# One level of Strassen's algorithm for the last two tiles of a first layer

## The chip, the cores and the metric

The kernel runs on one core of a Trainium2 chip. The metric is the device time of one execution in microseconds (us), as the median of several executions. TensorE (PE) multiplies matrices; VectorE (DVE), ScalarE (ACT) and GpSimd (POOL) work element by element; SyncE (SP) and ACT issue the DMAs. Each engine takes its own instructions strictly in the order in which the program lists them and waits for others by semaphores.

## The reference

Three blocks follow one another. An attention with a feature map gives `x`, 4608 rows of 512 numbers. The second block is the one that this change touches; the third has four more matrix products.

```python
def _moe_ref(x, w_in, w_out):          # x 4608 x 512, w_in 512 x 2048, w_out 2048 x 512
    h = x @ w_in
    g = h - np.tanh(h)
    return (g @ w_out).astype(np.float32)

def _moe2_ref(x, w1, w2, w3, w_out):   # w1, w2 512 x 1024, w3 1024 x 1024, w_out 1024 x 512
    a = x @ w1
    b = x @ w2
    h = a * b @ w3
    return (h @ w_out).astype(np.float32)
```

The weights come in double precision, and float32 accuracy is kept with TensorE's fast float32 format: each operand is split into a high part (the rounded number) and a low part (what the rounding lost), and each product is three matmuls, high by high, low by high, high by low.

## The kernel before

The program has three parts in a row: the attention, the "first layer" (`moe1`, the second block above) and the "second layer" (`moe2`, the third block, which already computes its products with one level of Strassen's algorithm, seven products of half-size blocks for eight; its lines are L840 and L849).

In the first layer all data stand transposed: features on the 128 partitions, tokens along the free axis. The 4608 tokens are nine tiles of 512 (`NB`), and the 2048 hidden features are sixteen blocks of 128 (`NFC`). A step `n` is one block of one tile, so the layer has 144 steps; step `n` is block `n % 16` of tile `n // 16`. In step `n` PE computes `h`, the product of block `n`'s input weights and the tile's x (`mm1`, L501: four slices of the 512 inputs by three matmuls, 12 matmuls of 512 columns), and then the output product of the block two steps earlier (`mm2`, L580: four output parts `y0` to `y3` by three, 12 matmuls of 512 columns that add up in four PSUM banks over the sixteen blocks). In most steps `mm2` takes the eight matmuls that need the high part `gh` first and the four that need the low part `gl` last; in the first and the last block of a tile it goes by output part, and `gl` is needed by the third matmul.

Between the two stands `act_g`: ACT squares `h`, takes its tanh, and makes two more operands for small arguments (L522 to L525); DVE forms `h - tanh(h)`, a polynomial and the choice between them (L529 to L533). `g_parts` then splits the result of the step before: ACT copies out `gh` (L550), and POOL subtracts it to give `gl` (L551). At the end of a tile (in the second step of the next) `y_out` copies the four finished banks to SBUF, three by ACT (L563) and one by DVE (L565), and they are stored to DRAM; the four copies share three buffers named `yo`.

Beside that, a table `extra` hands every step a share of other work: the conversion of weights from double precision (`conv`; POOL's part is L132), their split into two parts (`split`; POOL's part is L617), and for the second layer's first weights the sums that Strassen's algorithm wants (`combos`, eight groups, one every seven steps from step 14 on; POOL's lines L636 to L645). `pieces` converts the other two weights in 48 pieces over 54 steps. The next tile's x is loaded, multiplied by the attention's denominators and split in four slices (`load_x`, `mul_x` L1056, `split_x` L1063). In POOL's program the order within a step is: `gl` of the step before, then the step's share of `extra`, then the x work. What a step's POOL work delays is therefore the next `gl`.

The pool `ps_h` has three PSUM banks for `h`. SBUF arenas (`w`, `late`, `xa`, `xb`, `xn`) hold the weights' two parts, two tiles' x, and the x being prepared. In the last tile the second layer's weights (`w3t`, `wo2`) are loaded into slots as their blocks fall free, and `w34` (L738) begins the second layer while the last two `mm2` wait.

## Time and profile before

| | us |
|---|---|
| median of 3 executions (lowest to highest) | 1654.81 (1654.49 to 1658.12) |
| the profiled execution, its own time | 1654.07 |
| the profiled span, first to last instruction | 1652.3 |
| PE busy in it | 1641.5 |
| DVE, ACT, POOL busy | 1101.6, 935.2, 949.6 |

The time of an execution is the span and some 1.8 us around it. Busy is the time in which at least one instruction of the engine runs. PE's busy time is close to the span, but a matmul's recorded duration is longer than the distance between two of them, since they overlap; the distance is what counts. The first layer runs from 299 us to about 1084 us. TensorE's granted clock is at full speed (1.00) in all of it.

### The profile page before, as it was taken

To read this page: it belongs to the slowest core of one execution; us is meant where nothing else is said; L and a number is where in the kernel's file an instruction comes from. 1 tells how busy PE (TensorE), PEld (TensorE's weight loads), DVE (VectorE), ACT (ScalarE), POOL (GpSimd) and SP (SyncE) were. 2 spreads that over 40 slices of the span, in tenths; PEclk is the share of its full clock that TensorE was granted. 3 is DMA by queue.
4 is the path that set the end of the run, shared out by engine and by line. 5 is a ranking of instruction groups with operands and counts; after the bars stand their busy time and mean duration, and the time that the engine had idled before them with its cause. 6 is when DMAs were issued, how large, how long until landed. Compare 5 with 4: busy or idle time off the path is not lost.

```text
span 1652.3 us, 31982 instructions
## 1 busy us (share of the span) xinstructions
PE 1641.5 (99%) x11702; PEld 1356.1 (82%) x11702; DVE 1101.6 (67%) x1649; ACT 935.2 (57%) x1884; POOL 949.6 (57%) x948
## 2 busy tenths in 40 slices
PE   9999999999999999999999999999999999999999
PEld 7777776788888888888888888888888888889999
DVE  7888887697555555666666665536765756847574
ACT  6788877787767666767777765443232232312221
POOL 6888998596757565656565662254633624515241
PEclk9999999999999999999999999999999999999999
DMA  6566664332333333424353436429768777688886
GB/s 186 179 178 192 190 189 143 101 117 92 110 113 125 112 117 107 128 78 143 106 147 99 141 96 226 140 103 328 220 209 265 207 237 236 184 278 283 285 258 220
DMA packets 159788, 283.64 MB, mean 172 GB/s; under 512 B 20304, under 2 KB 48336, under 8 KB 159632
## 3 DMA queue, kind: packets, MB, share of 16 engines
q1 hardware_dynamic: 146800, 246.31, 47.7%
q10 hardware_dynamic: 12832, 35.30, 6.8%
q8 instruction: 92, 1.51, 0.4%
q14 instruction: 64, 0.52, 0.1%
HBM read 218.32 MB, written 63.21 MB: 170 GB/s over the span
## 4 chain that ended last, share of the span: by engine, by line
PE 91%; DVE 3%; ACT 3%; POOL 1%; DMA 1%; issue 1%; SPq 0%; ACTq 0%; DVEq 0%; POOLq 0%
PE y L580 22%; PE h L501 22%; PE q L840 15%; PE q L849 7%; PE pa L840 6%; PE kv L299 3%; PE o L849 3%; PE p L226 3%; PE o L356 3%; PE h L738 3%; PE o L365 1%; PE tr L266 1%; POOL ks L323 1%; ACT kp L248 1%; DVE dk L237 1%
## 5 line engine op out<-in xcount | busy, mean ns | idle before, releaser
L551 POOL TENSOR_TENSOR gl<-t,gh 128x512 fp32r<-128x512 f32 x144 | 187.0, 1298 | 242.0 <-ACT gh L550 155.2
L529 DVE TENSOR_TENSOR t<-h,t 128x512 f32<-128x512 f32 x144 | 99.3, 690 | 181.8 <-ACT t L523 174.6
L840 PE MATMUL q<-w,w 128*128 128x512 f32 (+1 forms) x960 | 210.8, 367 | 0.2 <-DVE c L912 0.2
L522 ACT ACTIVATE u<-h 128x512 f32<-128x512 f32 x144 | 85.7, 595 | 200.9 <-PE h L501 200.7
L840 PEld LDWEIGHTS q<-w,w 128*128 128x128 f32 x960 | 174.9, 188 | 23.7 <-DVE c L912 1.3
L580 PE MATMUL y<-gh,w 128*128 128x512 f32 x720 | 182.2, 390 | 0.6 <-ACT gh L550 0.6
L580 PEld LDWEIGHTS y<-gh,w 128*128 128x128 f32 x720 | 134.9, 188 | 29.8 <-ACT gh L550 1.0
L530 DVE SCALAR_TENSOR_TENSOR u<-h,u 128x512 f32<-128x512 f32 x144 | 99.4, 691 | 70.1 <-ACT m L525 70.1
L501 PE MATMUL h<-xa,w 128*128 128x512 f32 x600 | 143.9, 389 | 0.0
L902 ACT ACTIVATE c<-pa 128x512 f32<-128x512 f32 (+1 forms) x40 | 22.2, 556 | 194.8 <-PE pa L840 194.8
L501 PEld LDWEIGHTS h<-xa,w 128*128 128x128 f32 x600 | 112.5, 188 | 23.6 <-issue 0.2
L235 DVE TENSOR_REDUCE m<-p 128x4 f32<-128x512 f32 (+1 forms) x145 | 98.7, 681 | 36.9 <-PE p L226 31.9
L501 PE MATMUL h<-xb,w 128*128 128x512 f32 x480 | 115.4, 389 | 0.0
L533 DVE COPY_PREDICATED t<-m,s 128x512 f32<-128x512 uint32 x144 | 109.1, 757 | 4.9
L132 POOL TENSOR_TENSOR et<-et,eraw 128x256 uint32<-128x256 uint32 x104 | 77.9, 749 | 59.0 <-issue 38.6
L580 PE MATMUL y<-gh,late 128*128 128x512 f32 x432 | 111.1, 389 | 0.0
L501 PEld LDWEIGHTS h<-xb,w 128*128 128x128 f32 x480 | 90.1, 188 | 18.8
L525 ACT ACTIVATE m<-u,cs 128x512 f32<-128x512 f32 x144 | 104.0, 722 | 0.0
L524 ACT ACTIVATE s<-u,cs 128x512 f32<-128x512 f32 x144 | 100.2, 696 | 6.2 <-DVE t L533 6.2
L532 DVE SCALAR_TENSOR_TENSOR s<-s,u 128x512 f32<-128x512 f32 x144 | 100.7, 699 | 4.6
L580 PE MATMUL y<-gl,w 128*128 128x512 f32 x360 | 100.5, 390 | 1.1 <-POOL gl L551 1.1
L323 POOL TENSOR_TENSOR ks<-ks,kp 128x256 f32<-128x256 f32 x128 | 95.7, 774 | 9.2 <-ACT kp L248 9.1
(173 smaller groups left out, 3843.9 us busy)
## 6 DMA issues: line engine op xcount, KB each, us to landing
w<-w_d SPq DMA_DIRECT2D x420, 256.0 KB
w_d<-w SPq DMA_DIRECT2D x72, 256.0 KB
qk<-in_qk ACTq DMA_DIRECT2D x30, 576.0 KB
v<-in_v ACTq DMA_DIRECT2D x30, 320.0 KB
num_d<-st SPq DMA_DIRECT2D x128, 72.0 KB
xn<-num_d SPq DMA_DIRECT2D x36, 256.0 KB
eraw<-in_w SPq DMA_DIRECT2D x32, 256.0 KB
eraw<-in_w3t SPq DMA_DIRECT2D x32, 256.0 KB
```

The source lines that it names most:

```text
L323: POOL.tensor_tensor(s, kp[m // G][:, :, m % G, :] if t < 4 else s, x, ALU.add)
L501: PE.matmul(ps, a[:, kk, :], b[kk], start=m == 0, stop=m == 3 * NK - 1)
L524: ACT.activation(s, u, ACTF.Square, bias=c1_sb)
L525: ACT.activation(m, u, ACTF.Relu, bias=lim_sb, scale=-1.0)
L529: DVE.tensor_tensor(t, h, t, ALU.subtract)
L530: DVE.scalar_tensor_tensor(u, h, C2, u, ALU.mult, ALU.mult)
L532: DVE.scalar_tensor_tensor(s, s, C0, u, ALU.add, ALU.mult)
L533: DVE.copy_predicated(t, m.bitcast(U32), s)
L551: POOL.tensor_tensor(gl, t, gh.bitcast(F32), ALU.subtract)
L580: PE.matmul(yy[j][d], w[:, d * 128:(d + 1) * 128], x, start=i == 0 and m == 0, stop=i == NFC - 1 and m == 2,)
L840: PE.matmul(ps, w[:, a, c], x[b][:, kk, :], start=start and m == 0, stop=m == 5, skip_group_check=True)
L849: PE.matmul(ps, w[:, a, c], x[:, b, :], start=start and kk == 0 and n == 0, stop=kk == 3 and n == 2, skip_group_check=True,)
```

## The change

The first seven tiles are computed as before. Tiles 8 and 9 (`JA = 7` and 8 in the program's count) go by `pair`: two blocks at a time, 256 hidden features by 512 inputs by 512 tokens, with one level of Strassen's algorithm. Each of the seven products is 128 features by 256 inputs by 256 tokens, six matmuls of 256 columns (L885), so a pair has 42 matmuls of 256 columns where two steps had 24 of 512. The output products (`y_ops`, L816) stay 24 matmuls of 512 columns; they are kept in a list and issued in portions of 3, 8 and 13 between the products.

The seven sums of weight blocks are prepared during the first tiles by `combos_in`, eight groups, one every seven steps from step 18 on: two DVE additions, four POOL sums and four splits (ACT and POOL) for each, and ten stores to a DRAM buffer `win_d`. In the last two tiles `more_in` loads them back, 512 KB at a time, through a ring of five slots in the weights' own space. The x sums of these tiles are made by `next_x` (`mul` into `xb`, `sums_x`, `split_xk`). The products are added up by one ACT copy and five DVE additions per pair, into the banks X and Y of the three in `ps_h`; Z holds one product alone. The elementwise work of block Y is done within the pair; that of block X is finished in the next pair.

Other edits: `y3` is copied into the x buffer `xn` instead of `yo`, and the x load of a tile begins two steps later (steps 2, 5, 8, 11 of a tile, used two steps later); the 48 pieces are converted over 38 steps instead of 54, a step sooner each, and DVE instead of ACT makes their high parts; the last tile loads seven of the sixteen `w3t` slots during its pairs and nine after them, and one quarter of the second layer's first input last of all.

On PE, the tiles before and after; `h` is the x product's bank, `y_...` the four output banks. Before, one step:

```order
L501 MATMUL h<-xb,late 128x512 x12
L580 MATMUL y_12075<-gh,w 128x512 x2
L580 MATMUL y_12076<-gh,w 128x512 x2
L580 MATMUL y_12077<-gh,w 128x512 x2
L580 MATMUL y_12078<-gh,w 128x512 x2
L580 MATMUL y_12075<-gl,w 128x512
L580 MATMUL y_12076<-gl,w 128x512
L580 MATMUL y_12077<-gl,w 128x512
L580 MATMUL y_12078<-gl,w 128x512
```

And in the changed kernel about half a pair, from its first product on:

```order
L885 MATMUL hX<-late 128x256 x6
L885 MATMUL hZ<-late 128x256 x6
L816 MATMUL y_13456<-gl,w 128x512
L816 MATMUL y_13457<-gl,w 128x512
L816 MATMUL y_13458<-gl,w 128x512
L885 MATMUL hX<-late 128x256 x6
L885 MATMUL hY<-late,w 128x256 x6
L816 MATMUL y_13455<-gh,w 128x512 x2
L816 MATMUL y_13456<-gh,w 128x512 x2
L816 MATMUL y_13457<-gh,w 128x512 x2
L816 MATMUL y_13458<-gh,w 128x512 x2
L885 MATMUL hX<-xa,w 128x256 x6
```

The x products stand in groups of six narrow matmuls, with output products of the pair before between them.

On POOL, step 27, which holds a conversion (`et`), splits (`w`) and a slice of x (`xa`), up to the next `gl`. Before:

```order
L132 TENSOR_TENSOR et<-et,eraw 128x256
L617 TENSOR_TENSOR w<-et,w 128x256 x2
L642 TENSOR_TENSOR et<-et 128x256
L1063 TENSOR_TENSOR xa<-xn,xa 128x512
L551 TENSOR_TENSOR gl<-t,gh 128x512
```

And in the changed kernel, where `eraw` holds the input weights' sums:

```order
L137 TENSOR_TENSOR et<-et,eraw 128x256
L627 TENSOR_TENSOR w<-et,w 128x256 x2
L653 TENSOR_TENSOR et<-et 128x256
L691 TENSOR_TENSOR eraw<-eraw 128x256
L692 TENSOR_TENSOR eraw<-eraw 128x256
L627 TENSOR_TENSOR w<-eraw,w 128x256
L1334 TENSOR_TENSOR xa<-xn,xa 128x512
L556 TENSOR_TENSOR gl<-t,gh 128x512
```

Two sums and one split have come in ahead of the same `gl`.

On DVE, one step of tile 8 before (its last two rows are a piece's conversion):

```order
L529 TENSOR_TENSOR t<-h,t 128x512
L530 SCALAR_TENSOR_TENSOR u<-h,u 128x512
L532 SCALAR_TENSOR_TENSOR s<-s,u 128x512
L533 COPY_PREDICATED t<-m,s 128x512
L124 SCALAR_TENSOR_TENSOR et<-eraw,et 128x256
L121 TENSOR_SCALAR et<-et 128x256
```

And one pair in the changed kernel, from the second of its five sums on; `xb` and `xz` are its temporaries:

```order
L915 TENSOR_TENSOR xb<-hY,xb 128x256
L916 TENSOR_TENSOR hY<-hX,xb 128x256
L843 SCALAR_TENSOR_TENSOR s<-s,xz 128x512
L844 COPY_PREDICATED t<-m,s 128x512
L933 TENSOR_TENSOR hY<-hY,xb 128x256
L935 TENSOR_TENSOR hX<-hX,xb 128x256
L830 TENSOR_TENSOR t<-hY,t 128x512
L831 SCALAR_TENSOR_TENSOR xz<-hY,u 128x512
L843 SCALAR_TENSOR_TENSOR s<-s,xz 128x512
L844 COPY_PREDICATED t<-m,s 128x512
L830 TENSOR_TENSOR t<-hX,t 128x512
L831 SCALAR_TENSOR_TENSOR xz<-hX,u 128x512
```

The sums read PSUM banks, and the two rows on `hX` that release the bank for the next pair stand last, behind all of block Y's work.

The diff, cut:

```diff
+                elif d == 3:
+                    t = words_of("xn", 0, [512])
                 else:
...
-            def conv(src, into):
+            def conv(src, into, spare=True):
...
-                return [c[0], [], c[1] + c[2], c[3] + c[4] + [keep]]
-
-            def split(of, store):
+                return [c[0]] + [[]] * spare + [c[1] + c[2], c[3] + c[4] + [keep]]
+
+            def split(of, store, act=True):
                 o2 = {}

...
+                    if act:
+                        ACT.activation(w[:, 0], t, ACTF.Copy)
+                    else:
+                        DVE.tensor_copy(w[:, 0], t)
...
+            def combos_in(g, at):
+                both = [slots["in", 2 * g + i] for i in range(2)]
+                t = []
+
+                def whole():
+                    for hi, lo in both:
+                        raw = p2.tile([128, cw], I64, tag="eraw", name="eraw", bufs=4).bitcast(F32)
+                        DVE.tensor_tensor(raw, fc_view(hi).bitcast(F32), fc_view(lo).bitcast(F32), ALU.add)
+                        t.extend((raw[:, :cw], raw[:, cw:]))
+                    for q, i, half in ((0, 0, 0), (1, 0, 1), (3, 1, 1)):
+                        for e in range(2):
+                            SP.dma_start(win_d[7 * g + WHICH.index(q)][:, e], fc_view(both[i][e][:, 2 * half:2 * half + 2]).bitcast(F32))
+
+                def sums_1():
+                    POOL.tensor_tensor(t[3], t[2], t[3], ALU.add)
+                    POOL.tensor_tensor(t[2], t[0], t[2], ALU.subtract)
+
+                def sums_2():
+                    POOL.tensor_tensor(t[0], t[3], t[0], ALU.subtract)
+                    POOL.tensor_tensor(t[1], t[1], t[0], ALU.subtract)
+
+                def out(q, i, k):
+                    place(split(lambda: t[i], lambda w: SP.dma_start(win_d[7 * g + WHICH.index(q)], w)), at + k)
+
+                place([[whole], [sums_1], [sums_2]], at)
+                out(6, 2, 2)
+                out(4, 3, 3)
+                out(5, 0, 4)
+                out(2, 1, 4)
+
...
-                place(conv(src, t), at)
-                place(split(lambda: t[0], store), at + 5)
+                place(conv(src, t, False), at)
+                place(split(lambda: t[0], store, False), at + 4)
...
-                piece(*c, 70 + i * 54 // len(todo))
+                piece(*c, 70 + i * 38 // len(todo))
...
+            def more_in():
+                if blocks:
+                    t = words_of(*ring_at[ring_n[0] % len(ring_at)], [2, 2 * cw])
+                    ring_n[0] += 1
+                    n = blocks.pop(0)
+                    src = win_d[n:n + 2].rearrange("q p a n -> p q (a n)")
+                    SP.dma_start(t.bitcast(F32), src)
+                    ring.extend(t[:, q].rearrange("p (a n) -> p a n", a=2) for q in range(2))
+
+            def split_xk(j, k):
+                if (j - JA) % 2 == 0:
+                    t = words_of("w", k * 1024, [2, 512])
+                elif k < 4:
+                    t = words_of("late", 2048 + k * 1024, [2, 512])
+                else:
+                    t = words_of("xa", (k - 4) * 1024, [2, 512])
+                xk[j, k] = t
+                hi, lo = [t[:, e].rearrange("p (a n) -> p a n", a=2) for e in range(2)]
+                ACT.activation(hi, xk["s"][k], ACTF.Copy)
+                POOL.tensor_tensor(lo, xk["s"][k], hi.bitcast(F32), ALU.subtract)
+
+            xa = []
+
+            def next_x(j, i, acts=None):
+                if j + 1 == NB:
+                    return
+                if j + 1 < JA:
+                    if i % 3 == 2 and i > 2:
+                        split_x(j + 1, i // 3 - 1, xa[0])
+                    if i % 3 == 2 and i < 12:
+                        xa[:] = load_x(j + 1, i // 3)
+                    if i % 3 == 1 and i > 1 and i < 14:
+                        mul_x(*xa)
+                    return
+                for k in {7: (0,), 11: (4,)}.get(i, ()):
+                    split_xk(j + 1, k)
+                if i in (4, 6, 8, 10):
+                    POOL.tensor_tensor(raw_x(i // 2 - 2), xa[0], xa[1], ALU.mult)
+                if i in (2, 4, 6, 8):
+                    xa[:] = load_x(j + 1, i // 2 - 1)
+                if i in (9, 11, 12, 13):
+                    sums_x((9, 11, 12, 13).index(i))
+                for k in {12: (6,), 13: (2,), 14: (1, 3), 15: (5,)}.get(i, ()):
+                    split_xk(j + 1, k)
+
...
+                todo = [(d, m) for d in range(NK) for m in range(3)]
+                if first:
+                    todo.sort(key=lambda a: (a[0] // 2, a[1] == 2))
+                elif not last:
+                    todo.sort(key=lambda a: a[1] == 2)
+
...
+            def pair(n, ys):
                 j, i = divmod(n, NFC)
-                if n < n_all:
-                    mm1(n)
-                else:
-                    w34(n - n_all)
...
+                x1, x2 = extra.get(n, []), extra.get(n + 1, [])
+                X, Y, Z = [None] * 3
+                for k in ("XYZ", "YZX", "ZXY")[n // 2 % 3]:
+                    t = ps_h.tile([128, 512], F32, tag="h", name="h" + k)
+                    X, Y, Z = [t if k == q else o for q, o in zip("XYZ", (X, Y, Z))]
+                u2, u3 = [words_of("xb", 3584 + 256 * k, [cw]) for k in range(2)]
+                vb, va = [words_of("xz", 512 * k, [512]) for k in range(2)]
+
+                def product(ps, k, start=False):
+                    w, x = ring.pop(0), xk[j, k]
+                    m = 0
+                    for kk in range(2):
+                        for a, b in ((0, 0), (1, 0), (0, 1)):
+                            PE.matmul(
+                                ps, w[:, a, kk * 128:(kk + 1) * 128], x[:, b, kk * cw:(kk + 1) * cw],
+                                start=start and m == 0, stop=m == 5, skip_group_check=True,
+                            )
+                            m += 1
+                    used[0] += 1
+                    if used[0] % 2 == 0:
+                        more_in()
+
+                product(X[:, :cw], 0, True)
+                ACT.activation(u2, X[:, :cw], ACTF.Copy)
+                product(Z[:, :cw], 1, True)
+                y_some(3)
+                if n == n_a:
+                    g_parts(n_a - 1)
+                    stream.extend(y_ops(n_a - 1, False, True))
+                if left:
+                    g_parts(left["n"] + 1)
+                done = full.pop() if full else None
+                if done:
+                    for d in range(2):
+                        y_move(done, d, True)()
+                    store2 = y_move(done, 2, False)
+                DVE.tensor_tensor(u2, Z[:, :cw], u2, ALU.add)
+                product(X[:, cw:], 2)
+                product(Y[:, cw:], 3, True)
+                if left:
+                    left["sm"] = act_2(left["u"])
+                if done:
+                    store2()
+                DVE.tensor_tensor(u3, Y[:, cw:], u2, ALU.add)
+                DVE.tensor_tensor(Y[:, cw:], X[:, cw:], u3, ALU.add)
+                if done:
+                    y_move(done, 3, False)()
+                end_a()
+                spread(x1, True)
+                spread(x1, False)
+                next_x(j, i)
+                spread(x2, True)
+                spread(x2, False)
+                next_x(j, i + 1)
+                if left:
+                    g_parts(left["n"])
+                for a in ys:
+                    stream.extend(y_ops(*a))
+                y_some(8)
+                product(X[:, :cw], 4)
+                product(Y[:, :cw], 5)
+                DVE.tensor_tensor(Y[:, :cw], Y[:, :cw], u3, ALU.add)
+                product(X[:, cw:], 6)
+                DVE.tensor_tensor(X[:, cw:], X[:, cw:], u2, ALU.add)
+                ub, tb = act_1(Y)
+                sb, mb = act_2(ub)
+                dve_1(Y, tb, ub, vb)
+                dve_2(tb, vb, sb, mb)
+                ua, ta = act_1(X)
+                dve_1(X, ta, ua, va)
+                y_some(13)
+                if n == n_a or ys[-1][2]:
+                    full.append((j - 1, yy.pop(j - 1)))
+                tt[n + 1] = tb
+                left.update(n=n, u=ua, t=ta, v=va)
+
...
+            for n in range(n_a):
+                j, i = divmod(n, NFC)
+                if n == n_a - NFC:
+                    renew("xb")
+                    sums_x(4)
+                if n >= 18 and (n - 18) % 7 == 0 and (n - 18) // 7 < 8:
+                    combos_in((n - 18) // 7, n)
+                mm1(n)
+                act_g(n, mm2(n - LAG) if n >= LAG else None)
+                spread(extra.get(n, []), False)
+                for k in range({n_a - 6: 3, n_a - 4: 2}.get(n, 0)):
+                    more_in()
+                next_x(j, i)
+            renew("xz")
+            stream += y_ops(n_a - 2, False, False)
+            ys = []
+            for n in range(n_a, n_all, 2):
+                j, i = divmod(n, NFC)
+                pair(n, ys)
+                ys = [(n + 1, i == 0, False), (n, False, i == NFC - 2)]
+                if j + 1 == NB:
+                    if i == 2:
+                        load_b(0, ((0, 0), (0, 1), (1, 0)))
+                    if i >= 2:
+                        load_w3t(i // 2 - 1)
...
+            for i in range(7, NFC):
+                load_w3t(i)
+            load_b(0, ((1, 1),))
+            y_some(3)
+            g_parts(left["n"] + 1)
+            left["sm"] = act_2(left["u"])
+            end_a()
+            g_parts(left["n"])
+            w34(0)
+            for f in y_ops(*ys[0]):
+                f()
+            w34(1)
+            for f in y_ops(*ys[1]):
+                f()
+            for d in range(4):
+                y_out((NB - 1, yy[NB - 1]), d)
```

## Rows read from the trace of the kernel before

**Rows 1.** Page, parts 1 and 4: busy time by engine; longest chain by line.
```profile
span 1652.3 us, 31982 instructions
...
PE 1641.5 (99%) x11702; PEld 1356.1 (82%) x11702; DVE 1101.6 (67%) x1649; ACT 935.2 (57%) x1884; POOL 949.6 (57%) x948
...
PE y L580 22%; PE h L501 22%; PE q L840 15%; PE q L849 7%; PE pa L840 6%; PE kv L299 3%; PE o L849 3%; PE p L226 3%; PE o L356 3%; PE h L738 3%; PE o L365 1%; PE tr L266 1%; POOL ks L323 1%; ACT kp L248 1%; DVE dk L237 1%
```

**Rows 2.** Waits of PE, first layer: us in total, times, longest us.
```profile
PE y L580 <- POOL gl L551: 1.1, 2, 0.9
PE y L580 <- ACT gh L550: 0.6, 1, 0.6
```

**Rows 3.** Timeline, PE, a run of the x products: start us, us, instruction, xcount.
```profile
1004.93 2.88 PE L501 MATMUL h<-xa,w 128*128 128x512 f32 x12
```

**Rows 4.** Timeline, PE, 384 columns wide, second layer.
```profile
1500.42 2.24 PE L840 MATMUL q<-w,w 128*128 128x384 f32 x12
```

**Rows 5.** Groups by form: xcount | busy us, mean ns of one | idle us before.
```profile
L840 PEld LDWEIGHTS q<-w,w 128*128 128x128 f32 x960 | 174.9, 188 | 23.7 <-DVE c L912 1.3
L501 PE MATMUL h<-xa,w 128*128 128x512 f32 x600 | 143.9, 389 | 0.0
...
L840 PE MATMUL q<-w,w 128*128 128x384 f32 x384 | 72.0, 334 | 0.2 <-DVE c L912 0.2
...
L356 PEld LDWEIGHTS o<-qp,kvx 128*32 128x32 f32 x1024 | 32.9, 110 | 26.0 <-ACT st L376 1.1
...
L911 DVE TENSOR_TENSOR u<-q,u 128x512 f32<-128x512 f32 x24 | 16.6, 690 | 21.4 <-PE q L840 21.4
...
L911 DVE TENSOR_TENSOR u<-q,u 128x384 f32<-128x384 f32 x16 | 8.9, 557 | 9.5 <-PE q L840 9.5
```

**Rows 6.** Timeline, all engines, an undisturbed step of the first layer.
```profile
1029.61 0.60 ACT L522 ACTIVATE u<-h 128x512 f32<-128x512 f32 x1 [2.62 <-PE h L501]
1030.10 0.59 ACT L523 ACTIVATE t<-h 128x512 f32<-128x512 f32 x1
...
1031.81 0.63 ACT L550 ACTIVATE gh<-t 128x512 fp32r<-128x512 f32 x1
...
1032.56 1.30 POOL L551 TENSOR_TENSOR gl<-t,gh 128x512 fp32r<-128x512 f32 x1 [4.15 <-ACT gh L550]
1032.67 0.70 DVE L532 SCALAR_TENSOR_TENSOR s<-s,u 128x512 f32<-128x512 f32 x1
...
1033.41 0.74 DVE L533 COPY_PREDICATED t<-m,s 128x512 f32<-128x512 uint32 x1
...
1036.66 0.62 PE L580 MATMUL y<-gl,w 128*128 128x512 f32 x2
```

**Rows 7.** Timeline, POOL, steps 26 and 27.
```profile
443.32 1.31 POOL L551 TENSOR_TENSOR gl<-t,gh 128x512 fp32r<-128x512 f32 x1 [1.79 <-ACT gh L550]
445.40 0.74 POOL L132 TENSOR_TENSOR et<-et,eraw 128x256 uint32<-128x256 uint32 x1 [0.78 <-issue]
446.10 1.44 POOL L617 TENSOR_TENSOR w<-et,w 128x256 fp32r<-128x256 f32 x2
...
448.18 1.32 POOL L1056 TENSOR_TENSOR xn<-xn 128x512 f32<-128x512 f32 x1
449.44 1.32 POOL L551 TENSOR_TENSOR gl<-t,gh 128x512 fp32r<-128x512 f32 x1
...
455.22 1.29 POOL L551 TENSOR_TENSOR gl<-t,gh 128x512 fp32r<-128x512 f32 x1
```

**Rows 8.** Timeline, DVE, end of the second tile.
```profile
483.95 0.69 DVE L565 COPY yo<-y 128x512 f32<-128x512 f32 x1 [2.43 <-PE h L501]
```

**Rows 9.** Stretches of the first layer: us, busy us (x) by engine, PEclk, DMA, GB/s.
```profile
390.00:730.00 340.00, 339.11 (x1495) 280.22 (x1494) 201.29 (x330) 235.59 (x474) 212.84 (x224) 1.00 0.34 111
...
909.00:1084.00 175.00, 175.00 (x773) 144.72 (x772) 103.50 (x157) 108.65 (x210) 73.13 (x70) 1.00 0.47 148
```

**Rows 10.** Page, part 2: DMA throughput in 40 slices.
```profile
GB/s 186 179 178 192 190 189 143 101 117 92 110 113 125 112 117 107 128 78 143 106 147 99 141 96 226 140 103 328 220 209 265 207 237 236 184 278 283 285 258 220
```

More of the change, by code (lines that the diff above doesn't have):

```diff
@@ L51 @@
 FC_EARLY = 10
+JA = 7
+WHICH = (0, 5, 4, 6, 1, 3, 2)
 @with_exitstack
@@ L64 @@
     y_d = dram.tile([DM, NT], F32, name="y_d")
+    win_d = dram.tile([56, 128, 2, 256], F32, name="win_d")
     w12_d = dram.tile([8, 7, 128, 2, 256], F32, name="w12_d")
@@ new lines, in moe1, with dve_2, y_move @@
+            left = {}
+            def dve_2(t, v, s, m):
+                DVE.scalar_tensor_tensor(s, s, C0, v, ALU.add, ALU.mult)
+                DVE.copy_predicated(t, m.bitcast(U32), s)
+            def y_move(ys, d, act):
+                j, pss = ys
+                if d == 3:
+                    t = words_of("xn", 0, [512])
+                else:
+                    t = p1.tile([128, 512], F32, tag="yo", name="yo", bufs=3)
+                if act:
+                    ACT.activation(t, pss[d], ACTF.Copy)
+                else:
+                    DVE.tensor_copy(t, pss[d])
+                return lambda: ACT.dma_start(y_d[d * 128:(d + 1) * 128, j * 512:(j + 1) * 512], t)
@@ new lines, in moe1 @@
+            renew("xz")
[10 more added lines that the diff above has]
+                        load_w3t(i // 2 - 1)
+                    if 4 <= i < 12:
+                        for k in (i - 4, i - 3):
+                            slots["wo2", k] = two("wo", k, [DM])
+                            for e in range(2):
+                                SP.dma_start(slots["wo2", k][e].bitcast(F32), wo2_d[e][k])
```

106 lines of the change are left out of this document (68 added, 38 removed).

## Prediction

> **What bounds the kernel now.** I read the page first. PE is busy for 1641.5 of 1652.3 us, and the chain that ended last runs mostly along PE's own lines, L580 and L501 with 22% each [rows 1]. Then the waits of PE in the first layer: three waits, 1.7 us in 785 us [rows 2]. So the layer lasts as long as PE's queue of matmuls, and two things can move its end: the distance from one matmul to the next, and a new wait of PE. For the first I read the timeline of PE; for the second the slack that the other engines have in an undisturbed step, and how POOL used it in its fullest steps.
>
> The distance comes from runs of twelve. Twelve matmuls of 512 columns take 2.88 us with the last one's recorded length of 389 ns in it, so (2880 - 389) / 11 = 226.5 ns each [rows 3, 5]; twelve of 384 columns give (2240 - 334) / 11 = 173.3 ns [rows 4, 5]. The 128 columns between them cost 53.2 ns, which is 2.4 GHz (the granted clock is 1.00 here [rows 9]), and both have 13.2 ns on top of their columns. A step has 24 matmuls, 5.44 us.
>
> The slack: in an undisturbed step `gl` starts at 1032.56, ends 1.30 us later, and its first matmul starts at 1036.66, so POOL may be 2.80 us late [rows 6]. `gh` ends at 1032.44. In a tile's first and last block the third matmul already wants `gl`, not the ninth: six times 0.227 us less, 1.44 us.
>
> **The change part by part.**
>
> *The x products of the last two tiles.* No row has 256 columns. On the line through the two widths it is 106.7 + 13.2 = 119.9 ns. Bounds: 106.7 ns (nothing but the columns) and 173.3 ns (what 384 columns take). I take 120, the line's value, since both widths agree on what stands on top. A pair then has 42 x 0.120 = 5.04 us where two steps had 24 x 0.2265 = 5.44. That is 0.40 us in each of 16 pairs: **-6.4 us**. At the bounds it would be 0.95 us less or 1.84 us more per pair, -15 or +29 us; the break-even is 5.44 / 42 = 129.5 ns.
>
> What could lift it to the upper end is the weight load. Its recorded length falls from 188 to 110 ns between 128 and 32 columns [rows 5]: 0.81 ns a column, about 104 ns for 128, as long as a 256-column matmul streams. At 384 columns a load and a matmul together would be 104 + 160 ns, and the distance is 173: they overlap there.
>
> The Trainium skill, "TensorE: Matmul & The Clock Gate", under "Back-to-back issue gap", gives N / 2.4 + 2.5 ns for a warm matmul. By it (an estimate) 512 columns take 215.8 and 256 take 109.2 ns, and the change saves 0.59 us per pair, 9.5 us; the trace's 226.5 disagrees with it at 512 columns, and I go by the trace.
>
> *The elementwise work in a pair.* The narrowest place is bank X. Three banks turn, and the fourth product of the next pair (into Y) needs the X of this one, which DVE reads last. From the end of the sixth product's issue: 0.2 us until DVE sees it (389 - 227 ns of pipeline, and a few tens of ns); the addition of 256 columns, 0.42 us (690 ns for 512 and 557 for 384 [rows 5], so 424); the square of Y and its tanh (0.49 + 0.59 us [rows 6]): 1.75 us with the two hand-overs. Then DVE's six wide operations on Y and X at about 0.74 us each (1033.41 - 1032.67 [rows 6]): 4.45 us, 6.2 in all. ACT's path to X's tanh (1031.81 - 1029.61 = 2.20 us for Y's four operations, then 0.49 + 0.59 [rows 6]) is done earlier, at 3.95. PE in that time issues four products and 16 output matmuls: 4 x 0.72 + 16 x 0.2265 = 6.5 us. There is 0.3 us to spare, so in a regular pair I count nothing. The second pair of tile 8 has no output matmuls left for the portion of three (0.68 us): 0.4 us of wait. At the switch from steps to pairs the second product wants the bank of the step just done: its last reader ends about 3.2 us after that step's x product, PE arrives after 3.4; with ACT and DVE carrying conversions I give it 0.3. Together **+0.7 us**, with 0 and 6 as ends (0.3 us more in every pair is 5).
>
> *The input weights' sums in the first seven tiles.* This is the part that is hidden only as long as POOL keeps up. POOL is busy for 212.8 of 340 us there [rows 9], but in lumps. The fullest steps of before [rows 7]: four operations of 256 columns at (448.18 - 445.40) / 4 = 0.70 us, one of 512 at 1.26. The first conversion starts 2.08 us after a punctual `gl` has started (it waits for DVE), and the following `gl` starts 6.12 us after its predecessor instead of 5.44, the next one 5.78: 0.7, then 1.0 us late, well inside 2.80.
>
> The change adds two sums in the second step of a group, two sums and a split in the third, and splits later. In steps 26 and 27 POOL then has six and seven narrow operations and a wide one each: 2.08 + 6 x 0.70 + 1.26 = 7.5, 2.1 us late; then 2.1 + 1.3 (`gl` itself) + 7 x 0.70 + 1.26 = 9.5, 4.1 us late. PE stands for 4.1 - 2.8 = 1.3 us. By the POOL order, steps 61 and 62, 68 and 69 are the same: 3.8 us for the three groups. Steps 19 and 20, 54 and 55 (six, then seven and a wide one) and 40 and 41 (six and a wide one, then seven) end 2.8 late, just at the edge. Steps 47 and 48 end 1.5 late where 1.44 is allowed, and 33 and 34 lie at a tile's end: 0.3 for both. The two DVE additions per group can push the first conversion by up to 0.8 us: 0 to 5 us over the eight groups, and I take 1.0, since DVE idles for about 2 us per step. Sum 5.1 us; the ends are 3 and 10.
>
> *y's fourth part in the x buffer.* DVE's copy of y3 waited for a `yo` buffer (2.43 us idle before it at 483.95 [rows 8]), and everything behind it on DVE and POOL came late, up to the longest wait of PE, 0.9 us [rows 2]. `xn` is free at that point, and its next load comes after the store. I take the 0.9 us off: **+4.2 us** for the seven tiles. The later x loads have two steps instead of one to land; the 48 pieces in 38 steps put at most three narrow and two wide operations besides `gl` in a step (108), 1.3 us late at most. I count both as nothing, hidden by the 2.80.
>
> *The end.* PE's order there keeps the same work (24 matmuls before each of the last two output blocks). Nine weight loads and a quarter of the second layer's input come later, about 5.2 MB after the last product; at 220 to 285 GB/s [rows 10] they take 18 to 24 us, and the first of them is wanted after 22 us, the second layer's first products after 49. Nothing, since POOL, ACT and DVE have that long to catch up.
>
> **Sum.** -6.4 + 0.7 + 4.2 = -1.5 us on the profiled execution's own 1654.1, so 1652.6. The median of the runs shown lies 0.7 us above that execution, and I give **1653**. About 0.2% (3.3 us) is what a measurement of this kernel can tell from no change.
>
> **Rivals.**
>
> *POOL keeps up, and the gain stays.* If extra work starts sooner than 2.08 us after `gl`, or PE's lost time falls on waits that it has anyway, the stalls shrink to the present ones: -6.4 + 0.7 - 0.9 = -6.6, **1647.5**. For it speaks POOL's 63% in these tiles; against it that 14.2 us of queue in two steps of 10.88 cannot fit, whatever starts when. A chance of 0.33, also for a price of 256 columns below 120 and for half of this.
>
> *The chain over X decides.* The 6.2 us above have 0.3 us of cover. If nine hand-overs between engines, or narrow operations that are no cheaper than wide ones (0.69 for 0.42), bring it to 6.9, PE waits 0.4 us in each of 16 pairs at the fourth product: +6.4, **1659**, slower. It decides from 6.5 on. For it speaks that the rows of DVE are dependent and stand back to back; against it that the sum already has the wide operations at their full distance. 0.12.
>
> *Narrow matmuls are dear.* If the weight load shows and 256 columns take 150 ns, a pair costs 6.30 us: +13.8 + 4.9, **1673**. The Trainium skill, "TensorE: Matmul & The Clock Gate", says under "Measured speedup vs the span model", that a weight load overlaps a running matmul only in another row group; by that each would cost 104 + 107 = 211 ns, some 55 us in all, and the trace's 226.5 ns at 512 columns (104 + 213 would be 317) speaks against it. 0.06 for any price above 135.
>
> *The ring runs dry.* In four pairs of the last tile ring, `w3t` and `wo2` want 1.8 + 0.5 + 1.0 MB in 10.5 us, 320 GB/s; the busiest slice of before has 328 [rows 10]. At 285 the loads fall 1.2 us behind per pair, with about 8 us of lead in the ring. If the lead is spent, +5, **1658**. 0.04.
>
> **How the numbers follow.** 0.45 for the forecast, 0.33, 0.12, 0.06 and 0.04 for the rivals. The forecast's own range is 1650 to 1656 (3 to 10 us of stalls, 0 to 2 in the pairs). The range, 1647 to 1659, takes in the first rival and the second up to its price. Faster by over 0.2% (below 1651.5): most of the first rival and a little of the forecast, 0.35. Within it 0.45. Slower 0.20.
>
> **What would show it.** In the profile of the changed kernel: twelve of the 256-column matmuls should be 120 ns apart. PE's waits should name POOL's `gl` at steps 27, 62 and 69, above 1 us each, and no longer name the tile's end near 492 us. The pairs should be 10.5 us apart, with small waits at the second one of tile 8 and at the switch. The second layer should keep its length. I am wrong if the waits on `gl` stay below 2 us in all, if PE waits for DVE in every pair, or if the distance of narrow matmuls is not 115 to 125 ns.

## The result and the profile after

The changed kernel takes 1674.32 us (median of 4 runs, 1671.46 to 1677.02) against 1655.05 (1654.49 to 1658.12) for the kernel before: a ratio of 1.0114, with a 95% interval of 1.0099 to 1.0129. It is slower by 19 us, and outside the range of the prediction. The profiled execution is the slowest of the four, 1677.02 us. In the changed kernel's listing `mm1` is L506, `mm2` L587, `gh` L555, `gl` L556, the pairs' products L885, the second layer L1109 and L1118.

The page after, parts 1 and 4:

```profile
span 1675.2 us, 33193 instructions
...
PE 1645.3 (98%) x11990; PEld 1364.3 (81%) x11990; DVE 1167.6 (70%) x1795; ACT 943.6 (56%) x1888; POOL 1026.8 (61%) x1026
...
PE 75%; DMA 7%; ACT 6%; DVE 5%; POOL 4%; issue 2%; SPq 1%; ACTq 0%; POOLq 0%; DVEq 0%
PE q L1109 15%; PE h L506 9%; PE y L587 9%; PE q L1118 7%; PE pa L1109 6%; PE y L816 6%; DMA eraw<-in_w3t 4%; PE kv L304 3%; PE p L231 3%; PE o L1118 3%; PE o L361 3%; PE hX L885 3%; PE h L1008 3%; PE o L370 1%; PE hY L885 1%
```

Where the chain ran along the two lines of the first layer with 22% each [rows 1], they now have 9% each, and loads of a raw weight (`eraw<-in_w3t`), ACT, DVE and POOL stand between their matmuls. PE's waits in the first layer (us in total, times, longest us):

```profile
PE y L587 <- ACT gh L555: 10.3, 9, 3.2
PE y L587 <- POOL gl L556: 6.7, 8, 1.5
PE h L506 <- POOL xz L1334: 2.5, 2, 2.3
PE y L587 <- ACT yo L570: 0.3, 1, 0.3
```

1.7 us [rows 2] have become 19.8. A stop costs PE more than the wait that is listed. Here it stops for the last slice of x:

```profile
660.74 0.50 PE L506 MATMUL h<-xz,w 128*128 128x512 f32 x1 [2.27 <-POOL xz L1334]
661.07 2.00 PE L587 MATMUL y<-gh,late 128*128 128x512 f32 x8
```

The wait is counted from the recorded end of the matmul before, which lies 0.16 us after the point at which the next one starts in a running queue (389 against 226.5 ns [rows 3, 5]), and the second matmul starts 0.33 us after the first where 0.23 is usual. Together a stop costs about 0.27 us on top of its wait. So the 12.5 us of waits in steps 14 to 78, twelve stops, are about 16 us of time.

To see where they are I took, in each kernel's trace, the start of the first x product of steps 0, 14, 78 and 111 and of the second layer, and PE's last matmul. The distances in us, with the medians of the runs (e1 to e11 are the experiments below; the runs of before that stand beside them have medians of 1653.4 to 1655.3):

| kernel | 0-14 | 14-78 | 78-111 | 111 to second layer | second layer | median |
|---|---|---|---|---|---|---|
| before | 72.7 | 349.7 | 179.5 | 230.0 | 517.3 | 1655.1 |
| after | 72.0 | 365.8 | 190.0 | 224.7 | 517.3 | 1674.3 |
| e1 x back | 72.7 | 373.8 | 193.2 | 224.7 | 517.3 | 1686.7 |
| e2 pieces back | 72.1 | 364.6 | 179.5 | 244.7 | 517.3 | 1684.5 |
| e3 POOL only | 72.0 | 359.2 | 188.6 | 224.7 | 517.3 | 1668.5 |
| e4 hi only | 72.0 | 349.3 | 188.4 | 224.5 | 517.5 | 1656.2 |
| e5 loads first | 72.0 | 367.3 | 179.5 | 224.4 | 517.4 | 1664.8 |
| e6 spare step | 72.0 | 365.1 | 179.5 | 224.4 | 517.3 | 1666.0 |
| e7 sums on DVE | 72.1 | 352.6 | 189.5 | 225.5 | 517.3 | 1660.3 |
| e8 = e5 + e7 | 72.0 | 352.3 | 179.5 | 224.4 | 518.4 | 1652.4 |
| e9 hi on DVE too | 72.0 | 349.4 | 179.5 | 224.4 | 517.8 | 1650.5 |
| e10 four w | 72.0 | 349.7 | 179.5 | 235.6 | 517.3 | 1661.6 |
| e11 e8, x back | 72.8 | 354.4 | 180.7 | 224.4 | 517.5 | 1656.6 |

After against before: -0.7 + 16.1 + 10.5 - 5.3 + 0 = +20.6 us, where the medians differ by 19.3. Two stretches lose, and the pairs gain. What stands ahead of step 0 is not in the table: it is the same program in all rows, and step 0 begins at 297.6 to 304.5 us in these traces, so rows are better compared by stretch than by one execution's time.

The pairs gain about what was forecast. The timeline of PE (start us, us, instruction, xcount):

```profile
966.54 0.88 PE L885 MATMUL hX<-w 128*128 128x256 f32 x6
967.26 0.88 PE L885 MATMUL hZ<-w 128*128 128x256 f32 x6
```

Six matmuls of 256 columns follow six others after 0.72 us, 120 ns each. The Trainium skill, "TensorE: Matmul & The Clock Gate", "Back-to-back issue gap", gives N / 2.4 + 2.5 ns for the isolated gap of one matmul, which is 109.2 (an estimate); the trace has 11 more, as it had at 512 columns [rows 3].

**Steps 78 to 111.** PE's longest wait of the layer is here. The timeline around it, for SP's queue, ACT, POOL and PE (idle time before and what ended it in brackets):

```profile
873.97 0.32 SPq L708 DMA_DIRECT2D w3tl_d<-w  x1
874.38 0.91 SPq L708 DMA_DIRECT2D w3th_d<-w  x1
875.38 0.38 SPq L708 DMA_DIRECT2D w3tl_d<-w  x1
875.86 0.90 SPq L607 DMA_DIRECT2D eraw<-in_w3t  x2
...
880.69 0.43 ACT L123 ACTIVATE et<-eraw 128x256 f32<-128x256 f32 x1 [4.93 <-DMA eraw<-in_w3t]
882.10 0.43 ACT L123 ACTIVATE et<-eraw 128x256 f32<-128x256 f32 x1 [0.98 <-DMA eraw<-in_w3t]
882.44 0.58 ACT L527 ACTIVATE u<-h 128x512 f32<-128x512 f32 x1
...
884.62 0.62 ACT L555 ACTIVATE gh<-t 128x512 fp32r<-128x512 f32 x1
...
885.37 1.29 POOL L556 TENSOR_TENSOR gl<-t,gh 128x512 fp32r<-128x512 f32 x1 [5.69 <-issue]
...
885.29 3.54 PE L587 MATMUL y<-gh,w 128*128 128x512 f32 x8 [3.15 <-ACT gh L555]
```

Read it from the bottom. PE waits for `gh`. ACT makes it at 884.62, because it stood for 4.93 us before a conversion whose raw weights had not landed, and then for 0.98 more; the step's own square, tanh and `gh` come behind that in ACT's list. The two loads were issued at 875.86, 4.8 us earlier, and on SP they stand behind the stores of earlier pieces. Of each two stores the first waits for DVE's high part and the second for POOL's low part. SP's waits at these stores, from 299 to 935 us:

```profile
SPq L708 <- DVE et L129: 71.2, 23, 6.8
SPq L708 <- DVE w L623: 32.7, 10, 5.2
SPq L708 <- POOL w L627: 17.3, 30, 1.4
```

Most of this waiting ends with DVE, whose high part (L623, with L129 next in its list) comes behind the step's last elementwise operation; POOL's low part comes behind `gl`, and `gl` behind `gh`. So a late step makes the next loads late. That the stretch keeps itself late in this way is read from the order; e5 below cuts it at SP.

ACT's waits in this stretch (742 to 935 us) for those landings:

```profile
ACT et L123 <- DMA eraw<-in_w3t: 47.4, 27, 4.9
ACT et L123 <- DMA eraw<-in_wo: 7.9, 6, 2.4
```

**Steps 14 to 78.** POOL's timeline before PE's first long wait for `gl`, at 423 us:

```profile
414.20 1.50 POOL L556 TENSOR_TENSOR gl<-t,gh 128x512 fp32r<-128x512 f32 x1
415.66 0.75 POOL L137 TENSOR_TENSOR et<-et,eraw 128x256 uint32<-128x256 uint32 x1
416.36 1.44 POOL L627 TENSOR_TENSOR w<-et,w 128x256 fp32r<-128x256 f32 x2
417.75 0.74 POOL L653 TENSOR_TENSOR et<-et 128x256 f32<-128x256 f32 x1
418.46 0.74 POOL L691 TENSOR_TENSOR eraw<-eraw 128x256 f32<-128x256 f32 x1
419.27 0.74 POOL L692 TENSOR_TENSOR eraw<-eraw 128x256 f32<-128x256 f32 x1
419.97 0.74 POOL L627 TENSOR_TENSOR w<-eraw,w 128x256 fp32r<-128x256 f32 x1
420.67 1.29 POOL L1327 TENSOR_TENSOR xn<-xn 128x512 f32<-128x512 f32 x1
421.92 1.27 POOL L556 TENSOR_TENSOR gl<-t,gh 128x512 fp32r<-128x512 f32 x1
```

From one `gl` to the next 7.72 us pass (421.92 - 414.20) without a gap, where a step has 5.44. Three of the eight operations between them (L691, L692, and the L627 on `eraw`) are the new ones, and step 22 becomes 1.2 us longer. In the mean POOL is busy for 76% of this stretch (us, then busy us of PE, PEld, DVE, ACT, POOL, granted clock, DMA share, GB/s):

```profile
374.00:740.00 366.00, 353.20 (x1539) 287.16 (x1538) 231.00 (x371) 258.14 (x529) 278.53 (x301) 1.00 0.46 150
```

At the same time ACT waits for a `w` buffer, to put a high part into, whose last store has not landed (395 to 730 us):

```profile
ACT w L621 <- DMA win_d<-w: 28.8, 15, 2.5
ACT w L621 <- DMA w_d<-w: 11.5, 16, 1.9
```

### The profile page after: what moved, and what is told of

Same layout as the page of the kernel before. It is cut to its first block, busy times and chain, and to the rows that moved or that the text cites. A ratio compares the mean times of both kernels' runs of the same rounds, so it can differ in the third digit from the quotient of the medians.

```text
span 1675.2 us, 33193 instructions
## 1 busy us (share of the span) xinstructions
PE 1645.3 (98%) x11990; PEld 1364.3 (81%) x11990; DVE 1167.6 (70%) x1795; ACT 943.6 (56%) x1888; POOL 1026.8 (61%) x1026
## 4 chain that ended last, share of the span: by engine, by line
PE 75%; DMA 7%; ACT 6%; DVE 5%; POOL 4%; issue 2%; SPq 1%; ACTq 0%; POOLq 0%; DVEq 0%
PE q L1109 15%; PE h L506 9%; PE y L587 9%; PE q L1118 7%; PE pa L1109 6%; PE y L816 6%; DMA eraw<-in_w3t 4%; PE kv L304 3%; PE p L231 3%; PE o L1118 3%; PE o L361 3%; PE hX L885 3%; PE h L1008 3%; PE o L370 1%; PE hY L885 1%
## 5 line engine op out<-in xcount | busy, mean ns | idle before, releaser
L556 POOL TENSOR_TENSOR gl<-t,gh 128x512 fp32r<-128x512 f32 x144 | 187.6, 1302 | 202.6 <-ACT gh L555 140.8
L1109 PE MATMUL q<-w,w 128*128 128x512 f32 (+1 forms) x960 | 210.8, 367 | 0.2 <-DVE c L1181 0.2
L1109 PEld LDWEIGHTS q<-w,w 128*128 128x128 f32 x960 | 174.9, 188 | 23.6 <-DVE c L1181 1.3
L587 PE MATMUL y<-gh,w 128*128 128x512 f32 x560 | 144.0, 394 | 6.8 <-ACT gh L555 6.4
L587 PEld LDWEIGHTS y<-gh,w 128*128 128x128 f32 x560 | 105.4, 190 | 32.3 <-ACT gh L555 9.4
L555 ACT ACTIVATE gh<-t 128x512 fp32r<-128x512 f32 x144 | 90.1, 626 | 40.6 <-DVE t L844 37.2
L253 ACT ACTIVATE kp<-dk 128x512 f32<-128x512 f32 x144 | 82.7, 626 | 19.7 <-DVE dk L242 18.2
L627 POOL TENSOR_TENSOR w<-et,w 128x256 fp32r<-128x256 f32 x104 | 80.3, 786 | 21.4 <-DVE w L623 17.1
L231 PE MATMUL p<-wphi,qk 64*128 64x128 f32 x1152 | 90.0, 285 | 0.2 <-DVE dk L242 0.2
L231 PEld LDWEIGHTS p<-wphi,qk 64*128 64x128 f32 x1152 | 74.9, 187 | 18.7 <-issue 13.4
L506 PE MATMUL h<-xa,w 128*128 128x512 f32 x360 | 88.2, 389 | 0.0
L506 PE MATMUL h<-xb,w 128*128 128x512 f32 x360 | 86.6, 389 | 0.0
L587 PE MATMUL y<-gh,late 128*128 128x512 f32 x320 | 82.7, 391 | 4.0 <-ACT gh L555 3.9
```

The costliest lines, as they stand in the source:

```text
L231: PE.matmul(what[g][:, j, :], qk[st][r:r + 64, c], wphi[r:r + 64], start=True, stop=True)
L506: PE.matmul(ps, a[:, kk, :], b[kk], start=m == 0, stop=m == 3 * NK - 1)
L555: ACT.activation(gh, t, ACTF.Copy)
L556: POOL.tensor_tensor(gl, t, gh.bitcast(F32), ALU.subtract)
L587: PE.matmul(yy[j][d], w[:, d * 128:(d + 1) * 128], x, start=i == 0 and m == 0, stop=i == NFC - 1 and m == 2,)
L1109: PE.matmul(ps, w[:, a, c], x[b][:, kk, :], start=start and m == 0, stop=m == 5, skip_group_check=True)
```

## The experiments

The expectations count a stall to the step that it delays, one later than the text here.

**e1** undoes y's place and the x schedule in the first seven tiles:

```diff
-                elif d == 3:
-                    t = words_of("xn", 0, [512])
-                    if i % 3 == 2 and i > 2:
-                        split_x(j + 1, i // 3 - 1, xa[0])
-                    if i % 3 == 2 and i < 12:
+                    if i % 3 == 0 and i < 12:
                         xa[:] = load_x(j + 1, i // 3)
-                    if i % 3 == 1 and i > 1 and i < 14:
+                    if i % 3 == 1 and i < 12:
                         mul_x(*xa)
+                    if i % 3 == 2 and i < 12:
+                        split_x(j + 1, i // 3, xa[0])
```

> The changed kernel (1674.3 us) with one part undone: in the first seven tiles y's fourth part goes into a yo buffer again, and the next tile's x is loaded at steps 0, 3, 6, 9 and split at 2, 5, 8, 11 of each tile, as before. Theory A (losses come from engines that stand in order behind a late buffer or a late load; the late last x slice is one of them): TensorE's waits of 2.43 us (660.7) and 0.39 us (842.8) for x's last slice go, and the ACT and POOL work for x moves out of steps 64, 67 and 74; 1674.3 - 2.8 = 1671.5, down to 1669 if the late gl beside them goes too. Rival B (POOL has too much work in those steps, wherever x's part of it stands): the same POOL work is only moved, the stalls move with it: 1673.5 to 1675. In both, the DVE copy of y's fourth part waits some 2.4 us again at tile ends [rows 8].

Measured: 1686.71 us, 12.4 more than the changed kernel (11.9 by the table), and neither theory had that. The wait for x's last slice went, but the waits for `gl` rose to 14.0 us:

```profile
PE y L585 <- POOL gl L556: 14.0, 14, 2.3
PE y L585 <- ACT gh L555: 9.2, 10, 1.8
PE y L585 <- DVE yo L570: 3.3, 3, 1.7
```

So y's new place and the new x schedule, together, were a help. How the 12.4 us divide between the two was not tried; 3.3 us of waits are y's. That the rest is x's wide POOL operations meeting the sums is an argument here, which e11 tests.

**e2** puts the conversion of the second layer's weights back as it was:

```diff
-                place(conv(src, t, False), at)
-                place(split(lambda: t[0], store, False), at + 4)
+                place(conv(src, t), at)
+                place(split(lambda: t[0], store), at + 5)
-                piece(*c, 70 + i * 38 // len(todo))
+                piece(*c, 70 + i * 54 // len(todo))
```

> The changed kernel with the conversion of the second layer's weights put back: 54 steps instead of 38, one step between load and first use, hi part on ACT; the last 12 pieces then fall into the pair phase. Theory A (ACT stands behind the landing of the piece's load, 47.4 + 14.1 us of waits there, and gh and gl come late behind it): TensorE's waits from 819 to 935 us (gh 6.8, gl 0.7, and 1.6 at a low clock after the longest) go: 1674.3 - 9 = 1665, plus up to 2 in the pair phase for the pieces that come into it: 1664 to 1668. Rival B (the engines have too much work there: 48 pieces' ACT, DVE and POOL instructions are the load): per step the work falls by a third and the stalls go as well, but the work falls into the pairs, whose POOL and ACT are then late: 1668 to 1673. Rival C (the loss of this stretch is carried on from the stretch of combos_in): no change, 1673 to 1675.

Measured: 1684.47. Steps 78 to 111 are back at 179.5, so their whole loss comes from this edit, as A and B said and C did not. But the 12 pieces that now fall into the pairs cost 20.0 us there (224.7 to 244.7), far more than either gave. PE's waits there (from 925 us):

```profile
PE y L816 <- POOL gl L556: 9.2, 4, 4.6
PE y L816 <- ACT gh L555: 2.6, 2, 1.3
```

**e3** and **e4** take the sums of the first layer's input weights apart. e3 keeps POOL's work and leaves out the high parts on ACT and the `w` buffers; e4 keeps these and leaves out POOL's eight operations:

```diff
e3:
-                    place(split(lambda: t[i], ...), at + k)
+                    def s_lo():
+                        POOL.tensor_tensor(t[i], t[i], t[i], ALU.subtract)
+                        ...
+                    place([[s_lo]], at + k)
e4:
+                    def s_hi():
+                        w = p2.tile([128, 2, cw], F32R, tag="w", name="w", bufs=3)
+                        ACT.activation(w[:, 0], t[i], ACTF.Copy)
+                        ...
-                place([[whole], [sums_1], [sums_2]], at)
+                place([[whole]], at)
```

> The changed kernel with combos_in cut: whole, the four sums and four instructions of lo's size stay on DVE and POOL, but the hi copies on ACT and the use of the three w buffers are left out, and the four sums' blocks are stored from the weights' own tiles (other data, same bytes), so the first layer's last two tiles compute something else. Theory A (ACT waits for a w buffer whose store has not landed, 28.8 + 11.5 us of waits, and gh and then gl are late): TensorE's waits from 423 to 716 us other than x's (some 12 us) go: 1662 to 1664. Theory B (POOL's lumps as the prediction had them, only larger): the gl waits (7.6 us in that stretch) stay and only the gh waits (5.1) go: 1668 to 1671.

> The complement: in combos_in the four sums and the four lo subtractions on POOL are left out; whole, the hi copies on ACT, the w buffers and the stores (hi twice) stay, so the last two tiles of the first layer compute something else. Theory A (w buffers): the stores now start right after the hi copy and not after POOL's lo, so a part of the waits goes; some 6 of 12 us stay: 1666 to 1670. Theory B (POOL's lumps): the gl waits go, 7.6 us, and what of the gh waits follows from POOL holding w buffers: 1662 to 1667.

Measured: e3 1668.53, as theory B had it, and e4 1656.20, below both. With POOL's work alone 9.5 of the 16.1 us remain; without it nothing (349.3 against 349.7). PE's waits in steps 14 to 78 of e3, then those of e4 from 299 to 720 us (0.6 of its 0.8 us lie before step 14):

```profile
PE y L587 <- POOL gl L556: 5.2, 7, 1.4
PE h L506 <- POOL xz L1339: 2.1, 1, 2.1
PE y L587 <- ACT gh L555: 0.9, 1, 0.9
```

```profile
PE y L587 <- ACT gh L555: 0.8, 2, 0.6
```

My theory A, ACT behind the `w` buffers, falls as the main cause: it can explain what e3 took away, 6.6 us, and only on top of POOL's lumps (e3 leaves out the high parts' own time on ACT as well; e10 parts the two). x's late slice is a part of the lumps too, since e4 hardly has it. Steps 78 to 111 stay at 188.4 in e4, so the two losses are separate.

**e5** changes only an order: in each step SP gets the loads of pieces ahead of the stores. **e6** gives the pieces the empty step back that the change took.

```diff
e5:
+                early.update(c[0])
-                for f in fs:
+                for f in sorted(fs, key=lambda f: f not in early):
e6:
-                place(conv(src, t, False), at)
-                place(split(lambda: t[0], store, False), at + 4)
+                place(conv(src, t), at)
+                place(split(lambda: t[0], store, False), at + 5)
-                piece(*c, 70 + i * 38 // len(todo))
+                piece(*c, 70 + i * 37 // len(todo))
```

> The changed kernel (1674.3 us, 10.5 us of it lost in steps 78 to 111) with one order altered: in each step of the first seven tiles SP gets the loads of the second layer's weights ahead of the stores of that step, which wait for POOL. Same instructions, same work. Theory S (the loads stand on SP behind stores that wait for POOL's lo, so they land late, ACT waits for them in order, and gh and gl are late behind it): ACT's 61 us of waits for these landings shrink to under 20, the stalls of steps 93 to 111 fall from 10.5 to 2 to 5 us: 1666 to 1669. Rival D (48 pieces in 38 steps are simply too much work for ACT, DVE and POOL): no change, 1673 to 1676. Rival L (the loads themselves take too long for one step, whatever their place in the queue): a change of 1 to 3 us, 1671 to 1673.

> The changed kernel with one empty step between the load of a piece and its first use again (hi on DVE and the density stay, 37 steps instead of 38 so that the last one still ends in the seventh tile). Four eraw buffers hold 4 steps by 1.3 pieces = 5.2, so a load then waits on SP for a buffer. Theory S and rival L: ACT no longer waits for landings, 1665 to 1669, but for what the missing buffer keeps back, which may take 2 to 5 us of it again. Rival D: no change, 1673 to 1677.

Measured: 1664.78 and 1665.97, and in both steps 78 to 111 take 179.5 again. In e5 ACT's waits for the landings fall from 47.4 us to

```profile
ACT et L123 <- DMA eraw<-in_w3t: 2.1, 4, 0.7
```

and PE no longer waits between 742 and 925 us. Density (D) and the length of the load (L) fall: the same 48 pieces in the same steps cost nothing once their loads don't stand behind stores. A step more for the landing does the same. Steps 14 to 78, of which the edit touches only the last eight, are 1.5 us longer in e5's trace than in the changed kernel's: at 714 us a wait of 2.0 us (1.9 in the changed kernel) is followed by 3.4 us at a lower clock, of which the last section tells.

**e7** moves the four sums and the four low parts from POOL to DVE, **e8** is e5 and e7 together:

```diff
-                    POOL.tensor_tensor(t[3], t[2], t[3], ALU.add)
+                    DVE.tensor_tensor(t[3], t[2], t[3], ALU.add)
...
-                    place(split(lambda: t[i], lambda w: SP.dma_start(win_d[7 * g + WHICH.index(q)], w)), at + k)
+                    place(split(lambda: t[i], lambda w: SP.dma_start(win_d[7 * g + WHICH.index(q)], w), lo=DVE), at + k)
```

> The changed kernel with the four sums and the four lo subtractions of each combos_in on DVE instead of POOL; everything else as it is. Theory P (POOL's eight extra instructions of 0.74 us in five steps make gl late; leaving them out took the loss of steps 14 to 78 from 16.1 to -0.4 us): 16.1 falls to 0 to 4 us, 1674.3 - 14 = 1660, 1658 to 1663. Rival W (what helped in that run was that the stores went out right after the hi copy, so that the three w buffers came free sooner): lo still comes before the store, half of the loss stays, 1664 to 1670. Rival V (DVE is in the chain to gh, so its eight instructions of some 0.4 us only move the stall from gl to gh): 1668 to 1674.

> Loads first (e5) and sums and lo on DVE (e7) together. Theories S and P with no hidden third loss: the seven tiles lose 2 to 6 us, the pairs give 5.4 back: 1655 - 5.4 + 4 = 1653, 1650 to 1658, equal to the kernel before. Rival: the two losses share a cause (POOL late in both), so the second repair gives less than alone: 1656 to 1662.

Measured: 1660.30 and 1652.44. Of 16.1 us 2.9 remain in e7, so P holds, and W (half would stay) and V (the stall only moves) fall; e8 has both gains in full, and no third loss shows in the first layer (its trace has 1.1 us more in the second, which I did not follow up). What e8 still waits for in steps 14 to 78 is `gh`:

```profile
PE y L587 <- ACT gh L555: 1.5, 3, 0.7
```

**e9** moves the sums' high parts to DVE too, **e10** instead gives e8 a fourth `w` buffer and takes one `yo`, **e11** is e8 with e1's edit:

```diff
e9:  lo=DVE -> act=False, lo=DVE
e10: tag="w" ... bufs=3 -> bufs=4;  tag="yo" ... bufs=3 -> bufs=2
```

> e8 (1652.4 us) with the hi copies of combos_in on DVE too, so that nothing of combos_in is left on ACT. Theory A2 (what e8 still loses, 2.6 us in steps 32, 45, 67 and 74, is ACT standing for a w buffer with gh behind it): these waits go, 1652.4 - 2 = 1650.4, 1649 to 1651.5. Rival V (DVE then stands for the w buffer itself, and t, m and gh of the next step come late by the same time): no change, 1652 to 1654.

> e8 with a fourth w buffer, paid for with one of the three yo buffers. Theory A2: the 40 us of ACT's waits for stores fall to under 10 and TensorE's 2.1 us of gh waits with them, -2; against it y's third copy at a tile's end now waits for the first one's store, on ACT, up to some 0.5 us of TensorE's time at each of seven tile ends: 1650 to 1655, and the trace shows which. Rival (gh is late for another reason, the hi copies' own time on ACT): the gh waits at steps 32, 45, 67 and 74 stay, 1653 to 1656.

> e8 with y's fourth part in a yo buffer and x's loads and splits two steps earlier, as before the change (e1's edit, which cost 12 us where POOL was overfull). If e1's loss came from x's POOL work meeting the sums there, then with the sums on DVE this edit costs little: the waits at tile ends (1.2 + 0.5 + 0.3 + 0.2 us in steps 36, 8, 51, 10) come back, +2, and 0 to 2 more: 1654 to 1657. Rival (the x order itself, through SP's queue and the xn buffer, costs it): +8 to +12 again, 1660 to 1665.

Measured: e9 1650.52, e10 1661.62, e11 1656.57. e9 and e10 both bring steps 14 to 78 back to the length of before, and e10 does it with one more buffer and the copies still on ACT, so the rest of e8's loss was ACT behind the `w` buffers. e10 pays for it elsewhere than I said, in the pairs, where DVE's copies of y wait for a `yo` buffer:

```profile
PE y L818 <- DVE yo L857: 6.0, 2, 3.5
```

e1's edit cost 12.4 us on the changed kernel and 4.1 here, so the x order by itself is the smaller part of the loss. By the table 8.0 us of the loss in steps 14 to 78 have become 2.1, and there the meeting of x with the sums on POOL is what e8 takes away; 3.2 in steps 78 to 111 have become 1.2, where e8 differs in the order of the loads too.

e9 beats both kernels: ratio to before 0.9968 (0.9956 to 0.9980), 4.8 us. Its chain, part 4 of its page, is PE's again:

```profile
PE 95%; DVE 2%; ACT 1%; DMA 1%; issue 0%; SPq 0%; POOL 0%; ACTq 0%; DVEq 0%; POOLq 0%
```

## Why the prediction was wrong

*The x products and the pairs: right in the sum.* -6.4 + 0.7 = -5.7 was forecast, -5.3 measured; 120 ns is the line's value. The rivals on bank X, on narrow matmuls and on the ring did not occur. That the sum comes so close is in part luck: the waits of 0.7 us hardly show (no wait of PE is listed between 935 and 1120 us), but a regular pair takes 10.53 us where the terms give 10.48, since the output products among the narrow ones stand about 230 ns apart and not 226.5.

A weight load of 128 columns hides behind 256 columns, though both use all 128 rows: the distance is 120 ns, and the prediction's estimates for the two one after the other are 104 + 107. The Trainium skill ("TensorE: Matmul & The Clock Gate", "The mechanism"; the prediction names another heading) says that a load overlaps a running matmul only when the row group differs, and, above that, that a load into the background weight buffer is pulled ahead too. The 120 ns speak against the first for these matmuls; which buffer a load goes to no run here shows.

*The end: right.* The second layer has its 517.3 us.

Two steps failed, and either alone would have put the time above the range's 1659 (1653 + 10.5, or 1653 - 4.2 + 16.1).

*The first: "I count both as nothing, hidden by the 2.80".* The conversions cost 10.5 us, and x's last slice 2.6 of the 16.1 (the lumps make it late, since e4 and e7 hardly wait for it, and the new schedule leaves it no time). I had counted their operations per step against POOL's slack, and the conversions do fit, as e5 and e6 show. What I did not price is the wait that `conv(src, t, False)` adds: a load that must land one step sooner, on ACT's list ahead of `gh`, with SP's stores ahead of it. I asked how much work there is, and not what is queued behind a wait.

*The second: the sums, "Sum 5.1 us; the ends are 3 and 10", mis-sized.* Step by step the 16.1 us are these:

| steps | longer by, us | forecast, us |
|---|---|---|
| 29 and 71, which use the late `gl` of 27 and 69 | 3.5 | 2.6 |
| 64, which uses that of 62; PE stops there for x's last slice | 2.6 | 1.3 |
| 22, 36, 43, 50, 57, the other five groups | 4.3 | 1.3 (0.3, and the 1.0 for DVE) |
| 31, 37, 38, 44, 73 (waits for `gh`) and 66 (for ACT's copy of y) | 6.7 | 0 |
| 35, the tile's end near 492 us | -1.2 | -0.9 |
| elsewhere | 0.2 | 0 |

The mechanism was right for the first row, with waits of 1.5 us each and a stop's 0.27 on top, which the sum left out. Three of the other groups I had judged "just at the edge", with hand-overs of no length, and each of the five loses, step 22 alone 1.2. And ACT's waits for the three `w` buffers were not in the sum at all; e3, without them, has 6.6 us less.

*y's fourth part and the x schedule: right in sign, and too small.* Step 35 is 1.2 us shorter for 0.9, which is that wait with its stop, and 7 and 9 together 0.7; e1's edit gives that back.

*The rival "POOL keeps up", 1647.5,* is what the repaired kernel comes near to: 6.6 us were forecast for it, and e9 gains 4.8. The range's upper end allowed POOL at most 10 us; it had nothing for ACT standing before a buffer or a landing with `gh` behind it.

## What to carry to other kernels

When a step between a load and its first use is taken away, price the landing as a wait on the engine that uses it, and ask two things: what stands before the load on its queue, and what stands behind the use on its engine. POOL, three quarters busy in the mean of the stretch, was over the edge wherever its lumps met; compare the distance between two punctual operations with the step in every group, not in the worst ones only. Here twelve small operations per group on another engine, and loads put ahead of stores, turned 19 us of loss into 5 of gain.

## What was not expected of the hardware

After the wait of 3.15 us at 885 the next eight matmuls took 3.54 us, where twelve of the same width take 2.88 [rows 3]. The window from 885 to 889 us (us, then busy us by engine, granted clock, DMA share, GB/s):

```profile
885.00:889.00 4.00, 3.71 (x10) 2.96 (x11) 3.93 (x7) 4.00 (x10) 3.02 (x4) 0.57 0.12 39
```

A granted clock of 0.57 is mostly the lower level, 1.2 GHz; the 4 us after it have 1.00, and so have the 5 us before it, for 2.9 of which PE stood. So that wait cost PE about 1.6 us more than its length. The 20 us of e2 hold this as well: its ten waits in the pairs sum to 14.0, ten stops add some 2.7, and two stretches of 3.4 us at the lower level, after waits of 2.2 and 4.6 us, about 1.6 each, 20 together. How the 16.1 us divide between sums and low parts was not tried.
